# Weight scales one slot later, three of eight down units in the scores' PSUM ring: a re-laid schedule of a fused attention and GLU kernel

## The chip, the cores and the metric

The kernel runs on one core of one Trainium2 chip. The metric is the device time of one execution in microseconds (us). The engines are PE (matrix multiply, fed by its weight loads, PEld), DVE (VectorE), ACT (ScalarE), POOL (GpSimd) and SP (SyncE, which here only issues DMAs). Each engine works through its own instructions in the order of the program; an instruction that waits holds up everything behind it on its engine.

## The reference

```
xn = layernorm(x)                       # x: 2048 x 576
q, k, v = split(xn @ wqkv)              # 32 heads of 18
p = softmax(q k^T / sqrt(18), over keys 0..255 back)   # causal, window 256
s = (p v) @ wo
g = silu(((xn @ w_gate) * (xn @ w_up)) @ w_down)       # 576 -> 4608 -> 576
out = x + s * g
```

## The kernel before

Products are made of 16-bit halves: each operand is split into a high and a low float16 part, and two or three products are added. For that the weights are scaled by a power of two, taken from their largest absolute value, which is known only once they are loaded.

A prologue normalizes x and makes q, k and v. Then come 72 **slots**. A group g (0 to 17) is 256 of the 4608 hidden columns and takes four slots (`b = 4 * g` is its first): two halves k of 128 columns, two halves q of the tokens. In each slot PE makes the gate and up products of one (g, k, q) in the PSUM banks A and C (`prod`, `tail_`, line 844), and eight **down units** of an earlier group (`down`, line 908), which I call D0 to D7 in the order of the slot; each is six matmuls in one PSUM bank, and DVE adds it to `acc` at once (`down_out`, line 920). All down units use the one bank `dn`, so a down unit starts only when DVE has read the unit before it. The last 24 units use the four-bank ring `s`, which else holds the scores.

Beside that each slot from 1 to 64 carries one attention step s (a pair of heads on 512 queries): `score_pairs` (PE, line 715, four banks of the ring `s` twice a slot), `score` (DVE, 724), `probs` and `probs_hi` (ACT, 731 and 736), `turn_probs` (a subtraction on POOL, 745, and a DMA transpose on SP, 748), `weigh` (PE, 757), `finish` (DVE and POOL, 769 to 778). The loads of the next step's keys and queries and of v (`load_k`, `load_q`, `load_v`, lines 687, 694, 702) are on SP too.

The weights of group g go this way, with the slots counted from b:

- `ffn_raw` in slot b - 3 loads w_up (kind 1), w_down (kind 2) and w_gate (kind 0) (SP, 134, 136, 365; each has one buffer, `raw1`, `raw2`, `raw0`).
- `ffn_amax` takes the maxima of each half (DVE, 372).
- `ffn_spread_out` (DVE 377, then SP 124) writes the 128 partitions' maxima to DRAM (`sd_f`), and `ffn_spread_in` (SP 128) reads them back into every partition (`spread`).
- `ffn_scale` reduces them and makes the scales (DVE, 385 and 114 to 118; POOL, 387 to 389).
- `ffn_ratio`, `ffn_sums` (POOL, 393 and 404), `w_hi` (ACT, 139) and `w_lo` (DVE, 142) make the 16-bit parts `wg`, `wu`, `ws`; `dn_hi`, `dn_lo`, `dn_low` those of w_down (`dnw`).

`wo_raw`, `wo_amax`, `wo_out`, `wo_in`, `wo_scale` and `wo_split` do the same once for wo near the end. After slot 71 come the last down units and the output projection, `o_out`.

The order is written out by hand. Every call is entered with a slot and a time in it, and all calls are made in the order of these times; nothing waits for a time, it only orders the instructions on each engine. A slot is T = 18.65 of these units, the table `W` has the times that are not written beside their call, and times above T fall into the next slot:

```python
def at(slot, t, f, *a):
    todo.append((slot * T + t, len(todo), f, a))
...
for _, _, f, a in sorted(todo, key=lambda e: e[:2]):
    f(*a)
```

Of the kernel before, what the change touches and what calls it, by code (L numbers as in the profile page):

```python
# [20 lines left out]
def kernel(  # L21
# [11 lines left out]
    x = x[0]  # L33
# [11 lines left out]
    scale = DH ** -0.5  # L45
# [46 lines left out]
    def bank(name, bufs, shape=(128, 512), dt=F32):  # L92
        return psum.tile(list(shape), dt, name=name, bufs=bufs)
# [382 lines left out]
    a, b = TB.pop(0)  # L476
# [123 lines left out]
    for t in range(16):  # L600
# [17 lines left out]
        elif t in (3, 5):  # L618
            k = (t + 5) // 2 - 1
# [171 lines left out]

    NSLOT = NG * NCH
    T = 18.65
    W = {"ttr": [0.18, 0.51, 3.42, 3.58, 8.19, 8.27, 11.02, 11.23], "exp": [1.55, 4.0, 9.98, 11.48], "cast": [2.93, 5.11, 11.38, 12.78], "plo": [3.42, 6.27, 12.48, 13.36], "fin": 9.15, "whi": [6.07, 9.54, 10.52, 16.69], "wlo": [8.97, 12.85, 15.43, 16.76], "dhi": 17.01, "dlo": 18.36, "dlow": 18.98, "sum0": [7.91, 15.69, 20.69], "sum1": [-6.21, 0.74, 6.86], "amax": [13.45, 14.1, 14.89, 14.7, 17.23, 17.23], "scale": 7.11, "hhi0": 19.92, "hlo0": 21.75, "hhi1": 22.56, "hlo1": 24.61, "h1": 18.7, "pv": [17.2, 8.25], "x": 7.02}
    todo = []

    def at(slot, t, f, *a):
        todo.append((slot * T + t, len(todo), f, a))

    first_slot = 1  # L800
    for s in range(NSTEP):
        b = first_slot + s
# [3 lines left out]
        at(b - 1, 16.96, score_pairs, s, 0)  # L806
        at(b, W["x"], score_pairs, s, 2)
        for n in range(8):
            i, j = divmod(n, 2)
            at(b, W["ttr"][n], score, s, i, j)  # L810
        for i in range(4):
            at(b, W["exp"][i], probs, s, i)
            at(b, W["cast"][i], probs_hi, s, i)
            at(b, W["plo"][i], turn_probs, s, i)
            for j in range(2):
                at(b if i < 2 else b + 1, W["pv"][i // 2], weigh, s, j, i)
        at(b + 1, W["fin"], finish, s)
# [76 lines left out]
    DN = {}  # L894

    def down(u):
        g, r = divmod(u, 32)
        q, r = divmod(r, 16)
        par, r = divmod(r, 8)
        i, j = divmod(r, 2)  # L900
        ps = DN[u] = bank("dn", 1) if u < LATE else bank("s", 4)
        l = []
        for k in range(2):
            h, w = HH[4 * g + 2 * k + q, par], DW[g, k]
            for a, b in ((0, 0), (0, 1), (1, 2)):
                l.append((h[:, a, i * 128:(i + 1) * 128], w[:, b, j * HALF:(j + 1) * HALF]))
        for n, (a, b) in enumerate(l):
            nc.tensor.matmul(ps[:, :HALF], a, b, start=n == 0, stop=n == len(l) - 1)  # L908
# [12 lines left out]

    NDOWN = 32 * NG
    LAG = 2
    LATE = NDOWN - 24

    for g in range(NG):
        b = 4 * g
        if g > 0:
            for kind, t in ((1, 0.0), (2, 0.3), (0, 11.5)):
                for part in range(2):  # L930
                    at(b - 3, t + 0.1 * part, ffn_raw, g, kind, part)
            for n in range(6):
                at(b - 3, W["amax"][n], ffn_amax, g, (1, 1, 2, 2, 0, 0)[n], n % 2)
            at(b - 3, 18.2, ffn_spread_out, g)
            at(b - 2, 2.0, ffn_spread_in, g)
            at(b - 2, W["scale"], ffn_scale, g)
        for k in range(2):
            if g + k > 0:
                c = b if k else b - 2
                at(c, W["sum%d" % k][0], ffn_ratio, g, k)  # L940
                at(c, W["sum%d" % k][1], ffn_sums, g, k, 0)
                at(c, W["sum%d" % k][2], ffn_sums, g, k, 1)
                for what in range(4):
                    c = b + k if k and what == 0 else b + k - 1
                    at(c, W["whi"][what], w_hi, g, k, what)
                    at(c, W["wlo"][what], w_lo, g, k, what)
        for k in range(2):
            for f, t in ((dn_hi, "dhi"), (dn_lo, "dlo"), (dn_low, "dlow")):
                at(max(0, b + k - 1), W[t], f, g, k)
# [76 lines left out]

    b = NSLOT - 4
    for k in range(5):
        at(b, 2.5 * k, wo_raw, k)
        at(b, 2.5 * k + 10.0, wo_amax, k)  # L1030
        at(NSLOT - 2, 3.5 * k, wo_split, k)
    at(b + 1, 6.0, wo_out)
    at(b + 1, 10.0, wo_in)
    at(b + 1, 14.0, wo_scale)

    def banks(sl):
        BK["A"], BK["C"] = bank("up", 2), bank("up", 2)
# [1 line left out]
    def down_at(sl, n, t):  # L1039
        u = 8 * (sl - 3) + n - LAG  # L1040
        if 0 <= u < NDOWN:
            at(sl, t, down, u)
            at(sl, t + 0.75, down_out, u)

    for sl in range(NSLOT):
# [36 lines left out]
        at(sl, W["hlo1"], h_lo, sl, 1)  # L1082
    rest = range(8 * (NSLOT - 3) - LAG, NDOWN)
    for n, u in enumerate(rest):
        at(NSLOT, 0.75 * n, down, u)
        at(NSLOT, 0.75 * n + 0.74, down_out, u)
# [35 lines left out]
```

## Time and profile before

| | |
|---|---|
| median of three runs | 1699.5 us (1698.93 to 1700.48) |
| profiled execution | 1707.58 us, span 1705.9 us |
| mean granted PE clock | 0.984 |
| PE busy | 1602.6 us (94%) |
| DVE busy | 1328.7 us (78%) |
| ACT busy | 929.6 us (54%) |
| POOL busy | 791.2 us (46%) |
| mean busy share of the DMA queue that SP feeds | 57.0% of 16 engines |

The span is the time from the first to the last instruction. Busy shares are averages over the prologue (to about 190 us), the slots (to about 1630 us) and the output projection; what matters for a change in the slots is which engine has no idle time there, and what ends the idle time of that one. In the views below a row of the timeline has the start, the duration, engine, line, operation, out<-in and a count, and in brackets the idle time of the engine just before it and what ended that. A row of waits has the total, the number and the longest. A row of windows has for a stretch of time its length, the busy time of each engine with its count, the granted PE clock, the DMA share and GB/s.

### The profile page before, as it was taken

Reading aid. Unit: us, or ns where it says so; the run is one execution under the profiler, and the core shown is the slowest. Engines: PE = TensorE matmul, PEld = TensorE weight load, DVE = VectorE, ACT = ScalarE, POOL = GpSimd, SP = SyncE. Lnnn points to the kernel's source line nnn. Section 1 sums busy time; section 2 is a strip of 40 time slices with the busy share of each in tenths; the row PEclk is TensorE's granted clock in tenths of the full one; section 3 lists DMA queues with packets and bytes.
Section 4 is the critical chain, followed back from the end, with each engine's and each line's share of the span. In section 5 each row is a group of like instructions: output and inputs, shape, how many; then the busy total and the mean of one; then the engine's idle time right before and its main releaser. Section 6 shows DMA issues by size and latency. Waiting matters only on the chain.

```text
span 1705.9 us, 32395 instructions
## 1 busy us (share of the span) xinstructions
PE 1602.6 (94%) x11875; PEld 907.6 (53%) x11875; DVE 1328.7 (78%) x2989; ACT 929.6 (54%) x1742; POOL 791.2 (46%) x823
## 2 busy tenths in 40 slices
PE   8999879999998999998999999999999999989799
PEld 5455335555554555555555555555555555545477
DVE  6546568787888879797979897978888887956454
ACT  6433366565565656575756565666657565612220
POOL 3122345455464646564656555564646465622000
PEclk9999989999999999999999999999999999999999
DMA  9463255555646575666666675657575767520426
GB/s 229 124 192 109 83 99 126 95 128 78 138 81 142 112 147 115 131 125 118 134 125 139 125 150 103 145 98 147 100 162 101 153 113 149 116 62 1 99 58 180
DMA packets 551456, 206.06 MB, mean 121 GB/s; under 512 B 492544, under 2 KB 532096, under 8 KB 551296
## 3 DMA queue, kind: packets, MB, share of 16 engines
q1 hardware_dynamic: 551296, 203.98, 57.0%
q8 instruction: 93, 1.52, 0.4%
q14 instruction: 67, 0.55, 0.1%
HBM read 76.63 MB, written 23.75 MB: 59 GB/s over the span
## 4 chain that ended last, share of the span: by engine, by line
PE 54%; DVE 18%; DMA 10%; SPq 3%; issue 1%; POOL 0%; ACT 0%; DVEq 0%; ACTq 0%
PE up L844 29%; PE dn L908 17%; DMA spread<-sd_f 4%; DVE ws L142 3%; DVE acc L920 3%; PE pv L757 2%; DMA sd_f<-am 2%; DMA raw<-in_B_w_gate_dram 2%; DVE ft L876 2%; PE s L1012 2%; PE up L1012 1%; PE s L715 1%; DVE am L372 1%; DVE hh L892 1%; DVE dnw L142 1%; DVE ft L880 1%
## 5 line engine op out<-in xcount | busy, mean ns | idle before, releaser
L908 PE MATMUL dn<-dnw,hh 128*128 128x288 f16 x3312 | 501.0, 288 | 73.6 <-DVE acc L920 70.4
L908 PEld LDWEIGHTS <-hh 128*128 128x128 f16 x3456 | 330.2, 98 | 254.6 <-issue 109.7
L920 DVE SCALAR_TENSOR_TENSOR acc<-dn,sc,acc 128x288 f32<-128x288 f32 x520 | 266.5, 512 | 109.0 <-PE dn L908 108.1
L844 PEld LDWEIGHTS <-ws 128*128 128x128 f16 x1872 | 180.0, 99 | 192.4 <-issue 39.8
L844 PE MATMUL up<-XT,ws 128*128 128x512 f16 x1008 | 277.4, 386 | 0.3 <-DVE ft L876 0.3
L844 PE MATMUL up<-XT,wg 128*128 128x512 f16 x1008 | 254.6, 382 | 3.2 <-DVE ft L876 1.8
L884 POOL TENSOR_TENSOR ft<-ft 128x512 f32<-128x512 f32 x72 | 109.5, 1521 | 284.9 <-DVE ft L876 139.0
L844 PE MATMUL up<-TX,ws 128*128 128x512 f16 x864 | 216.0, 387 | 7.1 <-ACT ft L872 7.1
L888 ACT ACTIVATE hh<-ft 128x512 f16<-128x512 f32 x144 | 90.4, 628 | 240.8 <-DVE ft L880 236.7
L872 ACT ACTIVATE ft<-up 128x512 f32<-128x512 f32 x216 | 127.8, 592 | 170.9 <-PE up L844 165.8
L876 DVE SCALAR_TENSOR_TENSOR ft<-up,ft 128x512 f32<-128x512 f32 x216 | 147.8, 684 | 45.6 <-PE up L844 36.1
L844 PEld LDWEIGHTS <-wg 128*128 128x128 f16 x1008 | 99.3, 98 | 86.7 <-issue 6.7
L892 DVE SCALAR_TENSOR_TENSOR hh<-hh,ft 128x512 f16<-128x512 f16 x144 | 136.1, 945 | 1.2 <-ACT hh L888 1.2
L844 PEld LDWEIGHTS <-wu 128*128 128x128 f16 x720 | 71.0, 99 | 101.6 <-issue 40.1
L729 ACT ACTIVATE mx<-mx 128x2 f32<-128x2 f32 x256 | 51.0, 199 | 133.3 <-DVE mx L724 133.1
L339 PE MATMUL up<-XT,wq 128*128 128x512 f16 x504 | 111.4, 383 | 5.2 <-DVE qp L344 5.2
L844 PE MATMUL up<-TX,wu 128*128 128x512 f16 x432 | 106.7, 384 | 4.1 <-ACT ft L872 4.1
L757 PEld LDWEIGHTS <-pt 128*128 128x128 f16 x2880 | 86.1, 96 | 32.9 <-issue 17.5
L372 DVE TENSOR_REDUCE am<-raw 128x1 f32<-128x640 f32 (+1 forms) x108 | 80.8, 788 | 24.6 <-DMA raw<-in_B_w_gate_dram 24.6
L844 PE MATMUL up<-XT,wu 128*128 128x512 f16 (+1 forms) x288 | 100.0, 388 | 0.0
L757 PE MATMUL pv<-vt,pt 128*128 128x37 f16 x2880 | 93.4, 179 | 0.0
L142 DVE SCALAR_TENSOR_TENSOR ws<-sums,sc,ws 128x512 f16<-128x512 f32 x72 | 85.2, 1184 | 0.0
(1224 smaller groups left out, 2552.1 us busy)
## 6 DMA issues: line engine op xcount, KB each, us to landing
raw<-in_B_w_down_dram SPq DMA_DIRECT2D x36, 288.0 KB
raw<-in_B_w_gate_dram SPq DMA_DIRECT2D x36, 256.0 KB
raw<-in_B_w_up_dram SPq DMA_DIRECT2D x36, 256.0 KB
qk_d<-qp SPq DMA_DIRECT2D x112, 72.0 KB
vt<-v_d SPq DMA_DIRECT2D x48, 111.0 KB
ks<-qk_d SPq DMA_DIRECT2D x96, 54.0 KB
v_d<-vo SPq DMA_DIRECT2D x16, 296.0 KB
xr<-in_A_x_dram SPq DMA_DIRECT2D x16, 288.0 KB
```

Of the source, the lines that this page charges most:

```text
L142: nc.vector.scalar_tensor_tensor(w, rv, s, h, op0=OP.mult, op1=OP.subtract)
L339: nc.tensor.matmul(ps, a, b, start=i == 0, stop=i == len(pl) - 1)
L372: nc.vector.tensor_reduce(SC[g, "am"][:, half, kind:kind + 1], r, axis=AX.X if kind == 2 else AX.XY, op=OP.max, apply_absolute_value=True)
L757: nc.tensor.matmul(PVB[s][:, j, i, :VW], pt[:, 2 * nb * j + n], VT[s][:, lo_ + n % nb, j * VW:(j + 1) * VW], start=n == 0, stop=n == 2 * n ...
L844: nc.tensor.matmul(ps.rearrange("p (m n) -> p m n", n=128), w, b, start=start, stop=stop, skip_group_check=True)
L872: nc.scalar.activation(FT[sl, name], BK[bk], AF.Copy, scale=E_SC)
L876: nc.vector.scalar_tensor_tensor(f, BK[bk], E_SC, f, op0=OP.mult, op1=OP.add)
L884: nc.gpsimd.tensor_tensor(f, f, FT[sl, "a3"], op=OP.mult)
L888: nc.scalar.activation(hh[:, 0], FT[sl, ("a1", "a2")[c]], AF.Copy, scale=1.0 / LO)
L892: nc.vector.scalar_tensor_tensor(hh[:, 1], hh[:, 0], -LO, FT[sl, ("a1", "a2")[c]], op0=OP.mult, op1=OP.add)
L908: nc.tensor.matmul(ps[:, :HALF], a, b, start=n == 0, stop=n == len(l) - 1)
L920: nc.vector.scalar_tensor_tensor(d, ps[:, :HALF], SC[g][:, 9:10], d, op0=OP.mult, op1=OP.add)
```

## The change

The calls themselves do not change, apart from `down`, which takes three of its eight units in a slot (D0, D4 and D6) to the ring `s`. All else is times, and so the order on each engine.

```diff
-    W = {"ttr": [0.18, 0.51, 3.42, 3.58, 8.19, 8.27, 11.02, 11.23], "exp": [1.55, 4.0, ...], "cast": [2.93, ...],
+    W = {"ttr": [-1.02, -0.99, 2.9, 3.58, 7.44, 8.28, 9.7, 10.61], "exp": [0.73, 4.02, ...], "cast": [1.61, ...],
...
-        ps = DN[u] = bank("dn", 1) if u < LATE else bank("s", 4)
+        ps = DN[u] = bank("dn", 1) if u < LATE and (u + LAG) % 8 not in ON_S else bank("s", 4)
...
+    ON_S = (0, 4, 6)
...
-            for kind, t in ((1, 0.0), (2, 0.3), (0, 11.5)):
+            for kind, t in ((1, 0.0), (2, 0.3), (0, W["raw0"])):
...
-            at(b - 3, 18.2, ffn_spread_out, g)
-            at(b - 2, 2.0, ffn_spread_in, g)
+            at(b - 3, W["so"], ffn_spread_out, g)
+            at(b - 3, W["si"], ffn_spread_in, g)
             at(b - 2, W["scale"], ffn_scale, g)
...
-        at(b, 2.5 * k, wo_raw, k)
-        at(b, 2.5 * k + 10.0, wo_amax, k)
-        at(NSLOT - 2, 3.5 * k, wo_split, k)
-    at(b + 1, 6.0, wo_out)
-    at(b + 1, 10.0, wo_in)
-    at(b + 1, 14.0, wo_scale)
+        at(b - 1, 1.5 + 2.0 * k, wo_raw, k)
+        at(b - 1, 12.0 + 3.0 * k, wo_amax, k)
+        at(NSLOT - 2, 1.0 + 3.5 * k, wo_split, k)
+    at(b, 7.0, wo_out)
+    at(b + 1, 0.0, wo_in)
+    at(b + 1, 17.0, wo_scale)
```

The entries of `W` that the prediction speaks of, in the same units: `raw0` 11.5 to 11.17; the maxima `amax` from 13.45, 14.1, 14.89, 14.7, 17.23, 17.23 to 11.14, 11.93, 14.37, 14.25, 18.11, 18.75; `so` 18.2 to 21.83; `si` from 2.0 in the next slot to 24.97, which is 6.32 there; `scale` 7.11 to 14.47; the first half's ratio and sums `sum0` from 7.91, 15.69, 20.69 to 15.56, 19.68, 19.83; the last of the four `wlo` 16.76 to 18.08; `dlo` 18.36 to 18.02.

DVE at the end of slot 41 and the start of slot 42 (the slots b - 3 and b - 2 of group 11). The two maxima of w_gate are the rows on `raw` before `am<-am`; L880 and L876 are the slot's last two additions of gate and up products, L724 the scores of the attention step, L920 the additions of down units from the bank `dn` or `s`. Before:

```order
L920 SCALAR_TENSOR_TENSOR acc<-dn,sc,acc 128x288
L880 SCALAR_TENSOR_TENSOR ft<-up,ft 128x512
L372 TENSOR_REDUCE am<-raw_13392 128x1 x2
L876 SCALAR_TENSOR_TENSOR ft<-up,ft 128x512
L377 TENSOR_TENSOR am<-am 128x3
L920 SCALAR_TENSOR_TENSOR acc<-dn,sc,acc 128x288
```

Now:

```order
L876 SCALAR_TENSOR_TENSOR ft<-up,ft 128x512
L724 ISA sm__13480,mx<-s,bias,sig 128x384
L724 ISA mx 128x1
L724 ISA sm__13480,mx<-s,bias,sig 128x384
L724 ISA mx 128x1
L372 TENSOR_REDUCE am<-raw_13386 128x1
L920 SCALAR_TENSOR_TENSOR acc<-dn,sc,acc 128x288
L372 TENSOR_REDUCE am<-raw_13386 128x1
L920 SCALAR_TENSOR_TENSOR acc<-s,sc,acc 128x288
L724 ISA sm__13526,mx<-s,bias,sig 128x384
L724 ISA mx 128x1
L377 TENSOR_TENSOR am<-am 128x3
```

The maxima of w_gate moved behind L876 and the first two scores, the down units' additions stand between them, and the merge of the maxima, L377, is in the middle of the next scores.

SP at the same place: the last transposes of slot 41 and the stores of an attention output come first. Before:

```order
L748 DMA_TRANSPOSE pt<-pp 128x12x128 x2
L786 DMA o_d_85<-ob 128x4x144
L789 DMA o_d_85<-ob 128x4x144
L124 DMA sd_f_13490<-am 128x3
L128 DMA spread<-sd_f_13490 128x384
L748 DMA_TRANSPOSE pt<-pp 128x12x128
```

Now:

```order
L124 DMA sd_f_13537<-am 128x3
L748 DMA_TRANSPOSE pt<-pp 128x12x128
L687 DMA ks<-qk_d_80 36x768
L687 DMA ks<-qk_d_80 18x768
L687 DMA ks<-qk_d_80 36x768
L687 DMA ks<-qk_d_80 18x768
L748 DMA_TRANSPOSE pt<-pp 128x12x128
L128 DMA spread<-sd_f_13537 128x384
```

The read of the maxima, L128, which followed the write L124 directly, now stands behind two transposes and the four loads of keys.

DVE in slot 42 around the scale. Before:

```order
L876 SCALAR_TENSOR_TENSOR ft<-up,ft 128x512
L892 SCALAR_TENSOR_TENSOR hh<-hh,ft 128x512
L385 TENSOR_REDUCE sc<-spread 128x3
L114 TENSOR_SCALAR sc<-sc 128x3
L116 TENSOR_SCALAR sc<-sc 128x3
L117 RECIPROCAL sc<-sc 128x3
L118 TENSOR_SCALAR sc<-sc 128x3
L920 SCALAR_TENSOR_TENSOR acc<-dn,sc,acc 128x288
```

Now:

```order
L920 SCALAR_TENSOR_TENSOR acc<-s,sc,acc 128x288
L920 SCALAR_TENSOR_TENSOR acc<-dn,sc,acc 128x288
L385 TENSOR_REDUCE sc<-spread 128x3
L114 TENSOR_SCALAR sc<-sc 128x3
L116 TENSOR_SCALAR sc<-sc 128x3
L117 RECIPROCAL sc<-sc 128x3
L118 TENSOR_SCALAR sc<-sc 128x3
L920 SCALAR_TENSOR_TENSOR acc<-s,sc,acc 128x288
L880 SCALAR_TENSOR_TENSOR ft<-up,ft 128x512
```

The scale stood before the addition of D2; it now stands between the additions of D5 (from `dn`) and of D6 (from `s`), close to the slot's end.

More of the change, by code (lines that the diff above doesn't have):

```diff
@@ L793 @@
     T = 18.65
-    W = {"ttr": [0.18, 0.51, 3.42, 3.58, 8.19, 8.27, 11.02, 11.23], "exp": [1.55, 4.0, 9.98, 11.48], "cast": [2.93, 5.11, 11.38, 12.78], "plo": [3.42, 6.27, 12.48, 13.36], "fin": 9.15, "whi": [6.07, 9.54, 10.52, 16.69], "wlo": [8.97, 12.85, 15.43, 16.76], "dhi": 17.01, "dlo": 18.36, "dlow": 18.98, "sum0": [7.91, 15.69, 20.69], "sum1": [-6.21, 0.74, 6.86], "amax": [13.45, 14.1, 14.89, 14.7, 17.23, 17.23], "scale": 7.11, "hhi0": 19.92, "hlo0": 21.75, "hhi1": 22.56, "hlo1": 24.61, "h1": 18.7, "pv": [17.2, 8.25], "x": 7.02}
+    W = {"ttr": [-1.02, -0.99, 2.9, 3.58, 7.44, 8.28, 9.7, 10.61], "exp": [0.73, 4.02, 9.94, 10.85], "cast": [1.61, 4.85, 10.71, 12.76], "plo": [3.33, 6.32, 12.48, 13.35], "fin": 8.64, "whi": [6.17, 10.44, 7.03, 16.67], "wlo": [9.12, 13.19, 15.36, 18.08], "dhi": 16.48, "dlo": 18.02, "dlow": 18.26, "sum0": [15.56, 19.68, 19.83], "sum1": [-8.02, 0.5, 6.85], "amax": [11.14, 11.93, 14.37, 14.25, 18.11, 18.75], "scale": 14.47, "hhi0": 18.41, "hlo0": 22.9, "hhi1": 21.52, "hlo1": 23.66, "h1": 18.28, "pv": [16.98, 7.67], "x": 7.18, "raw0": 11.17, "so": 21.83, "si": 24.97}
     todo = []
```

## The prediction

> **What bounds the kernel now.** I read the waits of PE first, since it is busy almost throughout the slots, then the windows of one group's slots, then DVE, SP and the chain where PE waits. The waits of PE between 236 and 1647 us, and those of DVE that are on a DMA:
>
> ```profile
> PE dn L908 <- DVE acc L920: 70.4, 48, 7.6
> PE up L844 <- ACT ft L872: 4.1, 1, 4.1
> PE dn L908 <- DVE acc L918: 2.2, 4, 1.0
> ...
> DVE sc L385 <- DMA spread<-sd_f: 29.9, 17, 3.2
> DVE am L372 <- DMA raw<-in_B_w_gate_dram: 24.6, 13, 3.2
> DVE ps_o L976 <- DMA spread<-sd_wo: 8.4, 1, 8.4
> ```
>
> PE loses 77 us to waits, nearly all of it in down units that wait for the one bank `dn` to be read. DVE waits on DMAs about once a group for the loaded w_gate, once for the scales, and once for wo. Four slots in windows (length, busy PE, PEld, DVE, ACT, POOL, granted clock, DMA share, GB/s), and a stretch inside the last:
>
> ```profile
> 963.37:982.23 18.86, 18.86 (x156) 10.76 (x154) 17.18 (x38) 13.64 (x26) 10.99 (x11) 1.00 0.60 102
> 982.23:1001.47 19.24, 19.04 (x157) 10.76 (x155) 18.14 (x39) 13.80 (x26) 13.34 (x13) 1.00 0.56 97
> 1001.47:1020.57 19.10, 19.02 (x156) 10.75 (x154) 17.70 (x40) 12.32 (x23) 9.78 (x8) 1.00 0.74 183
> 1020.57:1045.25 24.68, 20.87 (x156) 11.21 (x154) 16.92 (x43) 11.15 (x21) 11.61 (x14) 0.93 0.76 127
> 1034.20:1037.60 3.40, 3.40 (x10) 1.16 (x9) 2.36 (x11) 2.38 (x5) 0.99 (x3) 0.50 0.76 151
> ```
>
> The first is a slot without a wait: PE is busy for all its 18.86 us, so this is the floor of a slot with attention. The last, slot 42, is b - 2 of group 11 and takes 24.68. Besides waiting, PE ran 3.4 us of it at half the clock, which costs 1.7 us (24.68 x 0.07). How the wait comes about, from DVE and PE of slots 41 and 42:
>
> ```profile
> 1018.99 0.69 DVE L880 SCALAR_TENSOR_TENSOR ft<-up,ft 128x512 f32<-128x512 f32 x1 [0.42 <-PE up L844]
> 1020.91 1.54 DVE L372 TENSOR_REDUCE am<-raw 128x1 f32<-128x640 f32 x2 [1.23 <-DMA raw<-in_B_w_gate_dram]
> 1031.28 0.66 DVE L385 TENSOR_REDUCE sc<-spread 128x3 f32<-128x384 f32 x1 [2.09 <-DMA spread<-sd_f]
> 1032.67 0.51 DVE L920 SCALAR_TENSOR_TENSOR acc<-dn,sc,acc 128x288 f32<-128x288 f32 x1
> ...
> 1033.23 0.90 PE L908 MATMUL dn<-dnw,hh 128*128 128x288 f16 x6 [2.24 <-DVE acc L920]
> ```
>
> Each wait of DVE for a DMA stands ahead of an addition L920, the next down unit cannot start, and PE stops, 2.24 us here behind the scale.
>
> **What there is to win.** 77 us of waits. For the clock, the view of cores has:
>
> ```profile
> core 0: 1705.9 us, clock 0.984
> ```
>
> That is 1705.9 x 0.016 = 27 us; some of it lies in the prologue, at the end and in idle time; I take 20 as coming from the stalls, with 0 as lower bound if the gate were to close for other reasons. Sum 97 us. The windows agree: slots 39 to 42 took 963.37 to 1045.25 = 81.9 us, 6.4 above 4 x 18.86, and 17 such groups would be 109; groups without half clock are cheaper.
>
> [...]
>
> **Step 1: the maxima of w_gate.** The loads stand at the same place in SP's order; the maxima move behind L876 and two scores. SP and the chain there, with the slot's clean PE rows for the deadlines:
>
> ```profile
> 1008.08 1.45 SPq L748 DMA_TRANSPOSE pt<-pp  x1
> 1009.58 1.89 SPq L687 DMA_DIRECT2D ks<-qk_d  x4
> 1014.97 0.40 SPq L702 DMA_DIRECT2D vt<-v_d  x1
> 1017.14 3.65 DMA raw<-in_B_w_gate_dram
> 1023.16 2.75 DMA sd_f<-am
> 1191.37 3.98 DMA spread<-sd_f
> 1509.06 5.62 DMA spread<-sd_f
> ...
> 963.37 1.46 PE L844 MATMUL up<-XT,wg 128*128 128x512 f16 x6
> 966.26 0.90 PE L908 MATMUL dn<-dnw,hh 128*128 128x288 f16 x6
> 977.03 0.90 PE L908 MATMUL dn<-dnw,hh 128*128 128x288 f16 x6
> 980.46 0.49 PE L715 MATMUL s<-ks,qs 54*128 54x384 f16 x4
> 980.88 0.78 PE L757 MATMUL pv<-vt,pt 128*128 128x37 f16 x24
> ```
>
> w_gate lands at 1020.79. L880 starts at 1018.99 as PE lets it; behind it now come L876 (0.60) and two scores (0.54 each), so the first maximum is reached at 1018.99 + 0.60 + 0.60 + 1.08 = 1021.3, after the landing even if the loads are no earlier. The 1.23 us of waiting go. D7's addition, which stands behind that maximum, is then over at 1021.3 + 0.77 + 0.43 = 1022.5; the next unit that needs `dn` is now D1, 2.89 us into the slot (966.26 - 963.37), here 1023.5. No wait is left.
>
> **Step 2: the scale.** In us from slot 42's start: L377 follows D7's addition (1.9) after 0.77 + 0.43 + 0.54, at 3.7, so sd_f is written by 3.8 + 2.75 = 6.6. SP passes a transpose, four loads of keys and a transpose before L128. What the transposes wait for comes from ACT and POOL:
>
> ```profile
> 1047.47 1.12 ACT L731 ACTIVATE sm__13785<-sm__13785,mx 128x384 f32<-128x384 f32 x2
> 1048.67 0.83 ACT L736 CAST pp<-sm__13785 128x768 f16<-128x768 f32 x1
> 1049.58 1.64 POOL L745 TENSOR_TENSOR pp<-sm__13785,pp 128x768 f16<-128x768 f32 x1 [1.48 <-ACT pp L736]
> ```
>
> Scores over at 0.7; 1.35 for the exponentials (1.12) with their bias ahead of them, an estimated 0.5 for a copy that stands between, 0.83 and 1.64: the first transpose at 5.1. With 1.45 and 1.89 the second could go at 8.5; its own scores are over at 4.3 and need 1.35 + 0.83 + 1.64, so 8.2 does not hold it. L128 goes at 8.6 + 1.45 = 10.1 and lands after 3.98 to 5.62, so at 14.1 to 15.7; I take 14.9, the middle. D5 starts at 13.66 (977.03 - 963.37), ends 0.74 later, and its addition is over at 14.9: DVE comes to L385 just when the data does. The scale takes 1.4 (1031.28 to 1032.67), D6's addition 0.43, so 16.7. The next that PE needs is the fourth score bank, which D6 now holds, at about 17.4 (980.46 - 963.37 and three scores). So the landing may be as late as 15.5 at no cost and costs one for one beyond. Nothing in the mean; 0 to 0.2 us a group.
>
> **Step 3: D0, D4 and D6 in `s`.** The rows to bound it by, in slot 44, where DVE is fullest:
>
> ```profile
> L142 DVE SCALAR_TENSOR_TENSOR dnw<-raw,sc,dnw 128x576 f16<-128x576 f32 x28 | 22.5, 802 | 0.0
> ...
> 1079.16 1.72 DVE L142 SCALAR_TENSOR_TENSOR ws<-sums,sc,ws 128x512 f16<-128x512 f32 x1
> 1080.80 0.51 DVE L920 SCALAR_TENSOR_TENSOR acc<-dn,sc,acc 128x288 f32<-128x288 f32 x1
> 1081.22 0.87 DVE L142 SCALAR_TENSOR_TENSOR ws<-sums,sc,ws 128x640 f16<-128x640 f32 x1
> ```
>
> `dn` is left with five units a slot and the waits for it in ordinary slots, which make 19.24 and 19.10 of 18.86, lose most of their cause: this is in the 77. Against that, a late D6 now holds back scores. D6's addition ends at 1081.22, 17.1 into a slot that starts at 1064.1 (1045.25 + 18.86), against the deadline of 17.4: 0.3 to spare. Cost 0; at most 0.3 us in two slots of four, 10 us in all.
>
> The last `w_lo` (0.87) and w_down's (0.80) now stand behind the next scores and ahead of D7's addition (0.43). With the scores over at 0.5 to 0.7 of the next slot it ends at 2.6 to 2.8, and D1 is due at 2.89. Cost 0; if this `w_lo` took 1.72 like its neighbour, up to 0.75 us in two slots a group, 25 us at most.
>
> **Step 4: POOL and SP in slot 43.** The five sums now stand together ahead of the first subtraction, the costliest and the cheapest of their five groups being:
>
> ```profile
> L404 POOL TENSOR_TENSOR sums<-sums,raw 128x256 f32<-128x256 f32 x36 | 31.8, 884 | 2.8
> L404 POOL TENSOR_TENSOR sums<-raw,raw 128x128 f32<-128x128 f32 x36 | 19.3, 537 | 0.0
> ```
>
> Three of the five stood there before. The two new ones are at most 2 x 0.88 = 1.8 us, and the subtraction at 1049.58, in slot 43, followed 1.48 us of idle time of POOL. So it slips by 0.3, and with it SP's transposes and the loads behind them, that of v last. In slot 41 v was loaded at 1014.97 - 1001.47 = 13.5 and its reader at 17.5 (980.88 - 963.37) did not wait. Cost 0; should 0.3 come through to PE, 5 us.
>
> **Step 5: wo.** The write and the read of its maxima in the chain:
>
> ```profile
> 1570.74 8.21 DMA sd_wo<-woa
> 1578.96 5.71 DMA spread<-sd_wo
> ```
>
> 14 us stood between `wo_out` and the data, and 8 units of schedule. Now `wo_out` is at 7.0 of slot 68, `wo_in` at 0 of 69 and `wo_scale` at 17 of 69: 28 units. The 7.6 us of PE, in the 77, go; the maxima (five, 0.74 each) fall into slots without attention, where DVE has room.
>
> **Sum.** Profiled: 1707.6 - 97 + 8, the 8 being half a microsecond for each group, a guess near the lower end of 0 to 40 us, which the bounds of steps 3 and 4 add up to: 1619. The profiled execution stands 8 us over the median. If that surplus stays, the median becomes 1611; if it was DMA waiting and goes with the stalls, up to 1618. I take **1614 us**.
>
> **The rivals.**
>
> *Part of it comes back* (0.23). For: DVE is busy 17.2 to 18.1 us of 18.86, so a late instruction is made good slowly, and step 2 has 0.6 us to spare. If SP's second transpose ends at 11.6, as in slot 41 (1009.58 + 1.89, then 1.45 and a gap), the spread lands at 16.4 and costs 0.9 a group, 15 us; with the 10 and 25 of step 3 up to 50, in place of the 8: 1628 to 1656. Against: that transpose was late through its scores, which now come 1.2 us earlier.
>
> *The wait only moves* (0.03). L128 slips by some 5 us, PE waits 4 to 6 us a group at the new place, 1696 to 1703. It needs two more transposes' worth of delay on SP; I see none in its order.
>
> *Slower* (0.05). D6's addition holds the ring `s` in every attention slot: PE's scores wait for it, and behind them the values' products and the next slot. It decides from 97 / 64 = 1.5 us a slot upward; at 2 us it gives 1699.5 - 97 + 128 = 1730. Against: the 0.3 us to spare in the fullest slot.
>
> *As forecast*: 1602 to 1628 (0.69); 1602 is nothing left over.
>
> 0.2% (3.4 us) is about what a measurement of this kernel tells from no change. Faster 0.92, same 0.03, slower 0.05. The range, 1602 to 1650, takes in the forecast and most of the first rival; with all bounds paid at once it would end at 1656.
>
> **What would show it.** Right: PE's waits for L920 below 15 us; no waits of L372 on w_gate; those of L385 below 5 us in all; slots of 18.9 us at b - 2; clock 0.99 or more; no wait of L976. Wrong: waits of PE's L715 or L908 on an addition from `s`; a wait of PE's L757; L385 waiting over a microsecond; many rows of 0.2 to 0.5 us at D1.

## The result, and the profile after

The changed kernel takes 1631.4 us (median of 4 runs, 1628.0 to 1632.7) against 1700.0 for the kernel before (4 runs, 1698.9 to 1701.2): ratio 0.9593, 95% interval 0.9577 to 0.961. That is 68.6 us less, 17 more than the forecast of 1614, inside the range and in the band of the first rival ("part of it comes back"). The profiled execution took 1631.2, with a span 76.4 us shorter than before's.

The view of cores, and the waits of PE between 236 and 1647 us, as in the prediction (total us, times, longest):

```profile
core 0: 1629.5 us, clock 0.993
```

```profile
PE dn L908 <- DVE acc L920: 14.0, 40, 0.7
PE s L715 <- DVE acc L920: 3.7, 8, 1.8
PE pv L757 <- DMA vt<-v_d: 0.8, 1, 0.8
PE dn L908 <- DVE acc L918: 0.7, 2, 0.4
PE up L844 <- DVE ft L880: 0.4, 1, 0.4
PE s L715 <- DMA qs<-qk_d: 0.3, 1, 0.3
```

The 77 us of waits are 20 now. Over the whole span PE's waits fell from 98 to 38 us and the time at half clock from 54.6 to 23.9 us, which is worth half of that, 15: together 75 of the 76.4. Between 236 and 1600 us DVE has no wait for w_gate left, and hardly one for the scales (over the whole span there is one of 1.2 us for w_gate, and the scales have five, 6.0 us in all):

```profile
DVE sc L385 <- DMA spread<-sd_f: 4.9, 4, 2.9
```

Where the 20 lie is seen in one group's slots, 27 to 30 (the same view as the prediction's windows: length, busy PE, PEld, DVE, ACT, POOL, clock, DMA share, GB/s):

```profile
692.02:711.75 19.73, 19.25 (x156) 10.83 (x154) 18.50 (x40) 14.25 (x26) 14.39 (x15) 1.00 0.55 100
711.75:731.63 19.88, 19.22 (x157) 10.84 (x155) 19.78 (x41) 13.45 (x25) 13.36 (x14) 1.00 0.50 100
731.63:750.37 18.74, 18.74 (x156) 10.76 (x154) 17.69 (x42) 11.78 (x22) 9.04 (x8) 1.00 0.81 197
750.37:769.83 19.46, 19.23 (x157) 10.74 (x155) 17.25 (x45) 11.04 (x21) 10.14 (x12) 1.00 0.83 139
```

The third is a clean slot, 18.74 us. The others (b - 1, b and b - 2) are 0.7 to 1.1 longer, and in slot 28 DVE is busy for 19.78 of 19.88 us. The places are two, here PE in slot 28 and, for the distance without a wait, in the clean slot 29:

```profile
719.68 0.76 PE L757 MATMUL pv<-vt,pt 128*128 128x37 f16 x24
720.99 0.90 PE L908 MATMUL dn<-dnw,hh 128*128 128x288 f16 x6 [0.55 <-DVE acc L920]
...
729.42 0.92 PE L715 MATMUL s<-ks,qs 54*128 54x384 f16 x4
...
739.55 0.76 PE L757 MATMUL pv<-vt,pt 128*128 128x37 f16 x24
740.15 0.90 PE L908 MATMUL dn<-dnw,hh 128*128 128x288 f16 x6
```

D3 comes 1.31 us after the values' products began instead of 0.60, as D2's addition is late: 0.71 lost, though the row says 0.55: in slot 29, where nothing waits, the rows of the two overlap by 0.16 (739.55 + 0.76 against 740.15). The four scores take 0.92 where the clean group takes 0.49 (the prediction's row at 980.46): the last waits for its bank, which D6 holds. I count such losses from start to start: the time from the start of the matmuls before a unit to its own start, less that time in slots where nothing waits. Over slots 18 to 64, D3 and D2 lose 14.4 us in all this way, and the eighth score 13.7.

Why D2's addition (720.43) and D6's (729.47, from `s`) are late shows in DVE and POOL of the same slot:

```profile
715.90 0.51 DVE L920 SCALAR_TENSOR_TENSOR acc<-dn,sc,acc 128x288 f32<-128x288 f32 x1
716.33 1.56 DVE L892 SCALAR_TENSOR_TENSOR hh<-hh,ft 128x512 f16<-128x512 f16 x1
717.82 0.68 DVE L876 SCALAR_TENSOR_TENSOR ft<-up,ft 128x512 f32<-128x512 f32 x1
718.42 2.08 DVE L892 SCALAR_TENSOR_TENSOR hh<-hh,ft 128x512 f16<-128x512 f16 x1
720.43 0.51 DVE L920 SCALAR_TENSOR_TENSOR acc<-dn,sc,acc 128x288 f32<-128x288 f32 x1
...
727.59 1.95 DVE L142 SCALAR_TENSOR_TENSOR ws<-sums,sc,ws 128x512 f16<-128x512 f32 x1
729.47 0.50 DVE L920 SCALAR_TENSOR_TENSOR acc<-s,sc,acc 128x288 f32<-128x288 f32 x1
...
714.20 0.73 POOL L404 TENSOR_TENSOR sums<-raw 128x256 f32<-128x256 f32 x1 [1.55 <-DVE ws L142]
715.01 0.74 POOL L404 TENSOR_TENSOR sums<-sums,raw 128x256 f32<-128x256 f32 x1
715.70 1.65 POOL L745 TENSOR_TENSOR pp<-sm__9454,pp 128x768 f16<-128x768 f32 x1
718.31 1.64 POOL L745 TENSOR_TENSOR pp<-sm__9504,pp 128x768 f16<-128x768 f32 x1 [0.96 <-ACT pp L736]
...
727.35 1.64 POOL L745 TENSOR_TENSOR pp<-sm__9628,pp 128x768 f16<-128x768 f32 x1 [0.53 <-ACT pp L736]
```

L892 takes 0.68 us where POOL does nothing beside it (13 rows of this trace, 0.677 to 0.684). Here the first starts inside POOL's L745 and ends 0.54 after it (717.89 and 717.35), and the second likewise (720.50 and 719.95): the multiplication is over only after POOL's instruction. L142, which makes D6's addition late, takes 0.74 for these 512 columns with no POOL instruction beside it (four rows, 0.736 to 0.750), and 1.95 here, again until 0.55 after POOL's (729.54 and 728.99). POOL has the first L745 so late because two sums L404 stand ahead of it: ACT's part, L736, was over at 714.96. The second L892 meets the next L745 only because the first was late.

### The profile page after: what moved, and what is told of

It is laid out like the page before. It is cut to its first block, busy times and chain, and to the rows that moved or that the text cites. A ratio compares the mean times of both kernels' runs of the same rounds, so it can differ in the third digit from the quotient of the medians.

```text
span 1629.5 us, 32463 instructions
## 1 busy us (share of the span) xinstructions
PE 1585.4 (97%) x11875; PEld 905.3 (56%) x11875; DVE 1360.3 (83%) x2989; ACT 923.2 (57%) x1742; POOL 815.0 (50%) x823
## 4 chain that ended last, share of the span: by engine, by line
PE 47%; DVE 29%; issue 4%; DMA 3%; ACT 2%; SPq 1%; POOL 0%; ACTq 0%; DVEq 0%; POOLq 0%
PE up L844 25%; PE dn L908 9%; PE s L908 6%; DVE acc L920 5%; DVE ws L142 4%; DVE ft L876 3%; PE pv L757 3%; DVE hh L892 3%; DVE wu L142 2%; PE s L1013 2%; DVE dnw L142 2%; PE s L715 2%; DMA raw<-in_B_w_gate_dram 2%; PE up L1013 1%; DVE am L372 1%
## 5 line engine op out<-in xcount | busy, mean ns | idle before, releaser
L908 PEld LDWEIGHTS <-hh 128*128 128x128 f16 x3456 | 329.1, 98 | 180.6 <-issue 25.5
L908 PE MATMUL dn<-dnw,hh 128*128 128x288 f16 x2070 | 310.3, 286 | 14.7 <-DVE acc L920 14.0
L844 PE MATMUL up<-XT,ws 128*128 128x512 f16 x1008 | 273.2, 381 | 1.2 <-DVE ft L876 1.2
L844 PE MATMUL up<-TX,ws 128*128 128x512 f16 x864 | 211.6, 381 | 6.1 <-ACT ft L872 6.1
L920 DVE SCALAR_TENSOR_TENSOR acc<-dn,sc,acc 128x288 f32<-128x288 f32 x325 | 166.1, 511 | 53.6 <-PE dn L908 53.0
L908 PE MATMUL s<-dnw,hh 128*128 128x288 f16 x1386 | 203.9, 286 | 0.0
L876 DVE SCALAR_TENSOR_TENSOR ft<-up,ft 128x512 f32<-128x512 f32 x216 | 147.4, 683 | 32.4 <-PE up L844 26.9
L884 POOL TENSOR_TENSOR ft<-ft 128x512 f32<-128x512 f32 x72 | 92.5, 1285 | 135.1 <-DVE ft L876 102.8
L892 DVE SCALAR_TENSOR_TENSOR hh<-hh,ft 128x512 f16<-128x512 f16 x144 | 149.9, 1041 | 0.2 <-ACT hh L888 0.2
L920 DVE SCALAR_TENSOR_TENSOR acc<-s,sc,acc 128x288 f32<-128x288 f32 x219 | 111.6, 510 | 27.2 <-PE s L908 27.1
L757 PEld LDWEIGHTS <-pt 128*128 128x128 f16 x2880 | 86.2, 96 | 47.6 <-issue 30.2
L757 PE MATMUL pv<-vt,pt 128*128 128x37 f16 x2880 | 93.4, 179 | 0.8 <-DMA vt<-v_d 0.8
```

Source lines behind the costliest of these rows:

```text
L757: nc.tensor.matmul(PVB[s][:, j, i, :VW], pt[:, 2 * nb * j + n], VT[s][:, lo_ + n % nb, j * VW:(j + 1) * VW], start=n == 0, stop=n == 2 * n ...
L844: nc.tensor.matmul(ps.rearrange("p (m n) -> p m n", n=128), w, b, start=start, stop=stop, skip_group_check=True)
L876: nc.vector.scalar_tensor_tensor(f, BK[bk], E_SC, f, op0=OP.mult, op1=OP.add)
L884: nc.gpsimd.tensor_tensor(f, f, FT[sl, "a3"], op=OP.mult)
L892: nc.vector.scalar_tensor_tensor(hh[:, 1], hh[:, 0], -LO, FT[sl, ("a1", "a2")[c]], op0=OP.mult, op1=OP.add)
L920: nc.vector.scalar_tensor_tensor(d, ps[:, :HALF], SC[g][:, 9:10], d, op0=OP.mult, op1=OP.add)
```

## The experiments

Each kernel is compared with the kernel before on the same chip. The kernels ran on several chips, on which the kernel before had medians of 1697.4 to 1701.3 us, so a difference between two of the kernels below can be off by some 3 us. "Start to start" counts are as above, over slots 18 to 64; rows of waits are for 236 to 1600 us.

| kernel | median us (range) | ratio to before, 95% |
|---|---|---|
| changed | 1631.4 (1628.0 to 1632.7) | 0.9577 to 0.961 |
| ring_undone | 1701.1 (1699.0 to 1702.7) | 0.999 to 1.0018 |
| before_ring | 1696.4 (1693.8 to 1699.9) | 0.998 to 1.0008 |
| before_ring_scores | 1693.8 (1688.3 to 1697.8) | 0.994 to 0.998 |
| ring_d0 | 1643.7 (1641.8 to 1646.9) | 0.9634 to 0.9701 |
| amax_back | 1654.1 (1652.1 to 1660.3) | 0.9703 to 0.9765 |
| wo_back | 1638.7 (1636.5 to 1640.9) | 0.965 to 0.9684 |
| d5_ring | 1622.3 (1618.5 to 1625.8) | 0.9511 to 0.957 |
| sums_late | 1612.2 (1611.8 to 1613.6) | 0.9456 to 0.9512 |
| sums_so | 1606.3 (1603.6 to 1609.0) | 0.9454 to 0.9488 |
| sums_so_d5 | 1607.1 (1604.0 to 1612.2) | 0.9455 to 0.9503 |

before_again is a second profile of the kernel before.

**ring_undone: the changed kernel without the ring.**

```
-    ON_S = (0, 4, 6)
+    ON_S = ()
```

> The changed kernel with all eight down units in the one bank dn again (ON_S empty), everything else as changed. Changed kernel: 1631.4 us. Theory 1 (the order of DVE was laid out for the ring; in dn the additions come too late): in slots b-1 and b the last w_lo and w_down's stand ahead of D7's addition, which then ends 2.66 us into the next slot while D0 is due at 1.30, 1.36 us lost in two slots a group; in b-2 a maximum stands ahead, 0.56; D6 waits for D5's addition, 0.3 to 0.8 in three slots. About 5 us a group, 16 groups, less the 14 us that the fourth score bank costs now: 1685 us, between 1670 and 1700, with PE's waits of L908 for L920 above 50 us. Rival (the ring brings little, since ordinary slots lost only 6 to 18 us before, and what the bank gives the scores take back): 1620 to 1640.

1701.1: the whole gain is gone, 70 us. Waits of PE, then DVE and PE at the start of slot 29 (762.29):

```profile
PE dn L908 <- DVE acc L920: 73.1, 78, 2.3
```

```profile
762.45 0.61 DVE L724 CUSTOM_DVE_ANT_0 sm__9739<-s,bias,sig 128x384 f32<-128x384 f32 x1
762.99 0.98 DVE L142 SCALAR_TENSOR_TENSOR dnw<-raw,sc,dnw 128x576 f16<-128x576 f32 x1
763.89 0.87 DVE L142 SCALAR_TENSOR_TENSOR ws<-sums,sc,ws 128x640 f16<-128x640 f32 x1
764.69 0.50 DVE L920 SCALAR_TENSOR_TENSOR acc<-dn,sc,acc 128x288 f32<-128x288 f32 x1
...
765.25 0.90 PE L908 MATMUL dn<-dnw,hh 128*128 128x288 f16 x6 [1.50 <-DVE acc L920]
```

Two scores and two splits stand ahead of D7's addition, and D0, due 1.3 us into the slot, waits for that. From start to start D0 loses 48 us. Theory 1 holds in its mechanism (its sign, waits of L908 above 50 us, is there), but its price was 16 us too low, and the time lies 1 us above its range.

**before_ring: the ring alone.** In the kernel before, `if u < LATE` became `if u < LATE and (u + LAG) % 8 not in ON_S` with ON_S = (0, 4, 6).

> The kernel before with D0, D4 and D6 of each slot in the ring s, and nothing else changed. Before: 1699.1 us; without the ring the changed kernel takes 1701.1, as long as before. Theory 1 (the parts need each other: the ring frees D0 from the wait behind the maxima, but the scores behind it and the wait of L385 for the scale at 7 us of slot b-2 stay, so that PE waits for scores or at D1 and D3 instead): of the 33.5 us that D0 lost in slots b-2 half goes, of the 28.4 us at D3 nothing; the time falls by 10 to 30 us, 1670 to 1690. Rival 1 (the ring alone is the gain, the moves of DVE's work bring nothing): 1630 to 1645. Rival 2 (nothing, the waits only move): 1694 to 1704.

1696.4, no change (rival 2). PE's waits:

```profile
PE s L908 <- DVE mx L724: 45.6, 46, 3.1
PE dn L908 <- DVE acc L920: 24.9, 15, 5.8
```

D0 no longer waits for D7's addition but for a score L724: the bank that it gets from the ring still holds scores, and in the order of before DVE reads them behind that addition. So the ring without the new times gives nothing, and all the new times together, the scores' place among them, give nothing without the ring (ring_undone).

**before_ring_scores: the ring and the scores' place.**

```
-"ttr": [0.18, 0.51, 3.42, ...
+"ttr": [-1.02, -0.99, 3.42, ...
```

> The kernel before with D0, D4 and D6 in the ring, and of the moved times only the first two scores of a slot (ttr -1.02, -0.99), so that they stand ahead of D7's addition. With the ring alone it took 1696.4 us; there D0 waited 45.6 us for those scores, whose bank it gets. Theory 1 (the ring and the place of the scores are one change in two parts; either alone gives nothing): the waits of D0 in slots b and b+1, 15.8 us over slots 18 to 64, go, and in b-2 0.6 us a group, where the maxima and their wait still stand ahead; 1665 to 1682. Rival (the losses stay with the maxima and the scale, and only change their place): 1690 to 1700.

1693.8, 7.5 us under the kernel before beside it (1701.3): the rival. The slots b and b + 1 did become clean (D0's 15.8 us there went, start to start), but DVE waits the more in b - 2. DVE's waits in before_ring, and then here, and PE's here:

```profile
DVE sc L385 <- DMA spread<-sd_f: 20.7, 13, 4.0
```

```profile
DVE sc L385 <- DMA spread<-sd_f: 40.2, 16, 4.1
DVE am L372 <- DMA raw<-in_B_w_gate_dram: 17.6, 13, 2.3
```

```profile
PE dn L908 <- DVE acc L920: 37.6, 17, 5.6
PE s L908 <- DVE mx L724: 23.7, 15, 2.7
```

In the mean of slots 18 to 63, the slots b and b + 1 became 0.71 and 0.68 us shorter than in before_ring (now 18.81 and 18.75) and the slots b - 2 0.83 longer (now 23.95). So some 60% of the gain is given back at the next wait for a DMA; L385's wait doubled. In the changed kernel, with maxima and scales behind their DMAs, it stays gained. No run moves the scales alone, so what their place brings by itself is not shown.

**amax_back: the maxima of w_gate at their old place in the changed kernel.**

```
-"amax": [11.14, 11.93, 14.37, 14.25, 18.11, 18.75]
+"amax": [11.14, 11.93, 14.37, 14.25, 17.2, 17.23]
```

> The changed kernel with the two maxima of w_gate back where they stood before, ahead of L876 of slot b-3 and the first two scores. Theory 1 (the prediction's step 1: it is the new place that took the waits away): L372 waits for w_gate again, 0.5 to 1.2 us a group, D7's addition and L876 are that late, and the time rises by 8 to 25 us, 1640 to 1656. Theory 2 (the load itself comes earlier: issued 12.5 us into the slot in the changed kernel, 14.0 before, as SP's transposes ahead of it go 1.6 us earlier): the data is there at 17 us, L372 at 17.9 hardly waits, and the time stays within 4 us of 1631.

1654.1, 22.7 us more: theory 1 in its size, and in its mechanism only in part. PE's waits, and DVE's for w_gate:

```profile
PE s L908 <- DVE mx L724: 12.7, 15, 1.5
PE s L715 <- DVE acc L920: 12.5, 19, 2.0
PE dn L908 <- DVE acc L920: 12.1, 32, 0.7
```

```profile
DVE am L372 <- DMA raw<-in_B_w_gate_dram: 6.3, 9, 1.1
```

L372 waits for 6.3 us in all, where it waited for 24.6 in the kernel before, since w_gate's load goes 12.5 us into its slot where it went at 14.0; in the changed kernel, for slot 41, which starts at 967.53:

```profile
980.04 0.48 SPq L134 DMA_DIRECT2D raw<-in_B_w_gate_dram  x1
```

Most of what D0 loses is the 1.5 us of the maxima themselves, ahead of the scores whose bank it needs: in the slots b - 2 it loses 0.6 to 0.7 us where L372 does not wait at all (3 of 12), and 0.8 to 1.6 where it does, 13.2 in all. The eighth score loses another 9 us in these slots (13.0 for 4.1). L385 waits longer there as well (9.6 us for 4.9), but how much of the 9 comes from that is not shown. Theory 2 is right on the load and wrong on the time.

**ring_d0: only D0 in the ring**, ON_S = (0,).

> The changed kernel with D0 alone in the ring: ON_S = (0,). With none there it took 1701.1 us, with D0, D4 and D6 1631.4. Theory 1 (the ring is needed for D0, whose turn comes while DVE still reads scores ahead of D7's addition): D0 lost 48 of the 57 us at down units without the ring (slots 18 to 64), D5 and D6 12; with D0 in the ring the 12 come back and the eighth score's 13.7 go: 1625 to 1640. Rival (D4 and D6 carry as much of it): 1650 to 1680.

1643.7, 4 us above the range of theory 1 and 6 below that of the rival. D0 carries 57 of the 70 us between 1701 and 1631, D4 and D6 the other 12; as theory 1 said, D5 and D6 lose 12.7 us again and the eighth score's losses go. The waits for L920:

```profile
PE dn L908 <- DVE acc L920: 26.5, 63, 1.0
```

**wo_back: wo's calls at their times of before** (the last part of the diff undone).

> The changed kernel with wo's loads, maxima, split, write, read and scale at their places of before. Theory 1 (the prediction's step 5): PE waits behind L976 again, about 8 us, and the time rises by 6 to 10 us above the changed kernel's 1631.4: 1637 to 1642. Rival (the wait of before came from the stalls ahead of it, or the tail hides it): within 3 us of 1631.

1638.7, 7.3 us more (10 when each is set against the kernel before beside it), theory 1. DVE waits for wo's maxima as it did before:

```profile
DVE ps_o L977 <- DMA spread<-sd_wo: 8.3, 1, 8.3
```

**d5_ring: D5 in the ring in place of D6**, ON_S = (0, 4, 5).

> The changed kernel with D5 in the ring s in place of D6: ON_S = (0, 4, 5). Counted from start to start of PE's matmuls, the eighth score of slots b-2, b-1 and b is late by 0.25 to 0.6 us, 13.7 us over slots 18 to 64, as D6 holds its bank. Theory 1 (a bank held too long): D5's addition is over 1.5 us before that score, so these losses go; D7 now waits for D6's addition, up to 0.3 us in two slots a group. 8 to 13 us less than the changed kernel's 1631.4: 1618 to 1623. Rival (DVE is simply full in these slots and PE waits for it at whatever comes next): within 3 us of 1631, with the loss at D7 or at the next slot's D1.

1622.3, 9 us less, theory 1. No score waits for an addition any more; D2's and D3's waits stay (13.4 us start to start, 14.4 in the changed kernel). A part does move on, as the rival said of the whole: D7 now loses 1.8 us and the next slot's D1 5.1, which lost nothing before.

**sums_late: POOL's sums behind the subtractions.**

```
-"sum0": [15.56, 19.68, 19.83], "sum1": [-8.02, 0.5, 6.85], "whi": [6.17, 10.44, 7.03, 16.67]
+"sum0": [15.56, 25.05, 25.5], "sum1": [-8.02, 6.4, 6.85], "whi": [6.17, 10.44, 10.52, 16.67]
```

> The changed kernel with POOL's sums L404 behind the second subtraction L745 of their slot instead of ahead of the first (sum0 15.56, 25.05, 25.5; sum1 -8.02, 6.4, 6.85), and the w_hi of the first sums back at 10.52. In the changed kernel L892 on DVE takes 0.68 us without POOL beside it, and 1.4 to 2.1 in slots b-1 and b, where L745 falls on it; D2's addition behind it is late and D3 waits 0.33 and 0.70 us, 10.6 us over slots 18 to 64. Theory 1 (work of POOL and of DVE on each other's time): the mean of L892 in slots b-1 and b falls below 1.0 us, the waits of D3 go, and the time falls by 8 to 14 us, 1617 to 1623. Rival 1 (DVE has too many instructions there, whatever POOL does): L892 gets shorter or not, the time stays within 3 us. Rival 2 (the sums now push the third and fourth L745 into w_lo L142): the D3 waits go, the eighth score's grow, -5 to +5 us.

1612.2, 19 us less, 5 beyond theory 1's range. L892 in all, of the changed kernel and then of this one (busy us, mean ns), and the windows of slots 27 and 28:

```profile
L892 DVE SCALAR_TENSOR_TENSOR hh<-hh,ft 128x512 f16<-128x512 f16 x144 | 149.9, 1041 | 0.2 <-ACT hh L888 0.2
```

```profile
L892 DVE SCALAR_TENSOR_TENSOR hh<-hh,ft 128x512 f16<-128x512 f16 x144 | 111.5, 774 | 0.3 <-ACT hh L888 0.3
```

```profile
689.13:707.88 18.75, 18.75 (x157) 10.76 (x155) 16.12 (x38) 14.30 (x26) 14.72 (x15) 1.00 0.51 89
707.88:726.69 18.81, 18.81 (x157) 10.76 (x155) 17.95 (x39) 13.50 (x25) 12.98 (x14) 1.00 0.63 123
```

POOL does the same work, DVE is 1.8 us less busy in slot 28, and both slots are clean: the waits of D3 went, and the eighth score's of slots b - 1 and b too, since D6's addition was late for the same reason: the L142 ahead of it, of 512 columns, takes 1.43 us in the median instead of 1.95. So DVE was not full of instructions: with POOL's sums at another place its L892 alone took 38 us less. (The edit also has ACT make the first sums' high part, `w_hi`, at its time of before, as the sums come later; that part was not run alone.) In b - 1 the mean of the first L892 is 1.23, above the 1.0 that was expected; it did not matter.

**sums_so: L377 one score earlier as well** ("so": 21.83 to 21.5).

> The kernel with the late sums (1612.2 us), and L377 one score earlier (so at 21.5): L377, three numbers a partition, takes 0.15 us without POOL beside it and 1.57 now, since L745 starts with it. Theory 1 (POOL's time on DVE's): L377 is back at 0.15 to 0.3 us, D2's wait in slots b-2 (4.1 us over slots 18 to 64) and most of the eighth score's there (4.1) go: 6 to 9 us less, 1603 to 1607. Rival (the L892 that follow now come onto the same L745 and stretch from 0.68 to about 1.5 in its stead): within 3 us of 1612.

1606.3, 5.9 us less, theory 1; 1.8 of it may be the chip, where the kernel before was that much faster. L377 of sums_late, then of this kernel:

```profile
L377 DVE TENSOR_TENSOR am<-am 128x3 f32<-128x3 f32 x18 | 19.8, 1100 | 0.0
```

```profile
L377 DVE TENSOR_TENSOR am<-am 128x3 f32<-128x3 f32 x18 | 3.2, 177 | 0.1
```

The mean falls from 1.10 to 0.18 us, D2's 4.1 us in slots b - 2 go and the eighth score's 4.1 there become 2.6. This kernel is 25 us under the changed one, the lowest median of all, and its slots are 18.75 to 18.81 in the mean but for b - 2, with 18.96.

**sums_so_d5: the same with D5 in the ring.**

> The kernel with the late sums and the earlier L377, and D5 in the ring in place of D6. Theory 1 (the eighth score's remaining losses are its bank, held by D6): the rest of the 4.1 us goes, and the time is 0 to 4 us under that of the kernel with D6 in the ring. Rival (with the additions on time D6 no longer holds anything back, and D7 now waits for D6 in slots b-2, where the scale's chain stands ahead of D6's addition): 0 to 4 us above it.

1607.1 against 1606.3, with ranges that overlap: neither theory is decided, and the time shows no difference between the two ways. In the profiled executions the eighth score loses 0.2 us instead of 2.7, but D1 5.0 instead of 1.4 and D3 3.3 instead of nothing; that execution was also the longest of its four (1612.2).

**before_again.** 

> The kernel before once more, for its profile. Its first profiled execution took 1707.6 us, 8 above the median, and the prediction left open whether that surplus stays in a median of the changed kernel. Theory 1 (chance of one execution, with DMAs that landed later): this one lies within 4 us of 1699, PE's waits for L920 below 70 us. Rival (it belongs to profiled executions of this kernel): 1705 or more.

The profiled execution took 1706.5 us, where 13 runs of it beside this one lie between 1692.8 and 1706.1, median 1701.3. So both profiled executions of the kernel before lie above the median, by 8 and 5 us, and that of the changed kernel 0.2 below. That is the rival's number, though PE's waits for L920 are 65.7 us, as theory 1 said. Against an effect of the profile on every kernel that waits for DMAs stands before_ring_scores: its DVE waits for 58 us on the scales and w_gate, and its profiled execution took 1692.1, below its median of 1693.8. What adds the 5 to 8 us stays open.

## Why the prediction was right, and where it was off

*The mechanism and the 97 us.* Right. The waits behind maxima and scales are nearly gone; the 77 became 20. The clock's 20 us (what the prediction calls the gate closing is a granted clock of 0.50 in the windows): from 236 us on, 44.4 us at half clock became 6.8, which is 18.8 us of time; the prologue, where the thirteen traces have anything from 7 to 20 us of half clock, took back 3.

*Step 1.* The outcome is right, the path is not. The step counted on no earlier load, but it goes 1.5 us earlier in its slot, as SP's transposes ahead of it do, and takes most of the wait away without any move of the maxima (amax_back). What the new place buys in the main is that the scores come ahead of the maxima. The step looked at D7's addition and D1; the deadline that counts is D0's, through the ring.

*Step 2.* Right in the main: 6.0 us of waiting for the scales over the whole span in place of 29.9. That is 0.35 a group on DVE, where the step had a cost of 0 to 0.2.

*Step 3.* The waits of `dn` in ordinary slots were taken for all that the ring brings. It brings 70 us, since the early scores push D7's addition behind D0's turn in three slots of four; the prediction did not price that, which cost it nothing as ring and scores were changed together. The bound for D6, 0.3 us in two slots of four and 10 us in all, was too low: 0.25 to 0.6 us in three slots, 13.7 us. The sign named for it, PE's L715 waiting on an addition, appeared. Of the splits ahead of D7's addition, the forecast (cost 0) held: D1 waits in no slot of 18 to 64.

*Step 4 is the one that failed.* It followed POOL's sums only into SP's transposes, 5 us at most. Their real way is POOL's L745 onto DVE's L892 and L142, and from there onto D2's and D6's additions: sums_late gives 19.2 us back, sums_so another 5.9 for L377, which the change had moved beside an L745 too. The durations in the prediction's own rows (L142 at 1.72 for 512 columns and at 0.87 for 640) were read as they stood, with no question what makes one long. In the changed kernel's trace the 64 L892 that start inside an L745 take 0.68 to 2.13 us and end 0.54 to 0.60 after it, and the 31 L142 from `sums` that do so take 1.47 to 2.08 and end 0.55 after it. The 24 L892 that start with POOL idle, and inside which an L745 starts, take 0.67 to 0.68. In ten of these the L745 has 512 columns and is itself long, 1.29 to 1.51, where the three of its size that start inside no L892 take 1.16. L920 and L876, with one input in PSUM, keep 0.50 to 0.52 and 0.67 to 0.69 throughout, also in the 201 and 79 rows beside an L745; whether it is the PSUM input that spares them was not tested.

*Step 5.* Right: 7.6 us forecast, 7.3 to 10 measured.

*The sum.* The term of 8 us for what is left over should have been 20 (waits from 236 us on), 12 of the 17 us that the median is above 1614. The other 5: the 8 us of surplus of the profiled execution were taken as staying in part, and went altogether, since 1631.2 is also the median. So 1618 was the number that followed, and with 20 for 8 it comes to 1630.6 for the profiled 1631.2. That the median lies in the first rival's band is not that rival's doing: of its three terms only the 10 us of step 3's D6 came (13.7 at the eighth score). DVE's waits for late scales are 6 us where it had 15, D1 lost nothing where it had 25, and the largest loss, the 14.4 us at D2 and D3, is in none of them.

*The signs.* Of those for right, the clock (0.993) came, and no wait for wo nor, from 236 us on, for w_gate. PE's waits for L920 are 17.7 us instead of below 15, L385's 6.0 in all instead of below 5, and the slots b - 2 take 19.4 us in the mean instead of 18.9. Of those for wrong, three appeared: waits of L715 on an addition, one of L757 (0.8 us), and one of L385 of 2.9 us; D1's short waits did not.

## What to carry to other kernels

Price a move on one engine by what it puts beside it on an engine that can hold it up, here GpSimd and VectorE (L892 takes 0.68 us alone and up to 2.13 beside an L745): list each instruction's shortest and longest time, and ask what runs beside the long ones before calling an engine full. Two edits that each measure as nothing, here the ring and the new times, can be the whole gain together, when each moves the wait to the place that the other clears; so undo parts from the finished version rather than only adding them one by one. Time gained ahead of a wait for a DMA can be largely given back there, here some 60% of it, as long as the consumer stands ahead of the DMA's landing.

## What was not expected of the hardware

PE's half clock comes in stretches of 3.41 us (41 of 51, the rest 6.83) in the thirteen traces, from 236 to 1600 us, and a wait's length goes only with the odds of one: of recorded waits of PE of 0.8 to 1.6 us 1 in 85 had one beside it (begun between 3.5 us ahead of the wait's end and 5 behind), of 1.6 to 2.0 6 in 33, of 2.0 to 2.4 9 in 21, of 2.4 to 3.2 14 in 18, above that 15 in 18. So ring_undone, with as much waiting as before (73 us) but in pieces of up to 2.3, kept this clock:

```profile
core 0: 1697.3 us, clock 0.994
```
